# An attention and feed-forward kernel with its weight decode partly moved to GpSimd, 14 scratch slots and a new order of steps

## The chip, the core and the metric

The kernel runs on one core of a Trainium2 chip. The metric is device time in microseconds of one execution, the median of several runs. The engines are TensorE (PE in the profile; its weight loads are PEld), VectorE (DVE), ScalarE (ACT) and GpSimd (POOL); SyncE (SP) issues the loads, ScalarE the stores.

## The reference

Two stages follow each other, all in 32-bit floats. The first is chunked attention over 4 batches, 8 heads, 768 positions, head size 64, with 8 memory keys in front of every window:

```python
for c in range(nc):                     # chunks of 32 queries
    k_full = concat(mem_k, k[l_start:r_end])   # 16 left, 8 right of the chunk
    v_full = concat(mem_v, v[l_start:r_end])
    a = softmax(scale * q_c @ k_full.T)
    out[c] = a @ v_full
x = out as 3072 tokens x 512
h = x @ w_in                            # 512 x 1024
solu = h * softmax(h)
ln = (solu - mean) / sqrt(var + 1e-6) * g_ln
return ln @ w_out                       # 1024 x 512
```

The two weight matrices arrive as 64-bit floats; the host hands them over as pairs of 32-bit words, and the kernel decodes them itself.

## The kernel before, in words

The 3072 tokens are 24 tiles of 128. A unit is one tile (units 0 and 1) or two (units 2 to 12). The program is a list of steps, the string ORDER, read from left to right; a step name is a kind, its number (unit, tile, piece, with a part behind a point) and, behind @, an engine: V VectorE, S ScalarE, G GpSimd, Y SyncE. Each engine executes its steps in the order of that list and waits where data or a buffer are not there. Nothing else sets the order.

**Weights.** w_in is eight pieces (0 to 7, piece 2c + h is row block c, half h), w_out eight (8 to 15). D loads a piece of 512 KB (L268) into a slot. A (ScalarE, L274) unpacks the high words, B and E (VectorE, L279, L284) shift and mask them to a float and its power of two, H rounds the float into w_in_h or w_out_h. T (VectorE, L301) turns the low words into a float:

```python
nc.vector.scalar_tensor_tensor(t, word(i, 0), factor, p, ALU.mult, ALU.mult)
```

that is integer word times 2^-52 times the power of two. R adds float minus rounded float plus low part on TensorE with three products by an identity matrix (L309, L310, L311), and W (ScalarE) copies the sum to w_in_l. Some w_out pieces are instead scaled, subtracted and added on GpSimd or VectorE (K L319, Y L324, J L328).

**Attention, per unit.** Lq, Lk, Lv load q, k and v (L236). S (TensorE, L400) makes the scores, M the negative row maximum (L422), Bm subtracts it (L431), X is the exponential (ScalarE, L440), Z the row sum and its inverse (L444 to L448). The probabilities are turned on TensorE and copied out (PT L380, PC) or by a transposing transfer with a split into 16-bit halves before and a join after it (Ps, Px L361, Pm; copies of L221 on ScalarE and L223 on GpSimd). V multiplies by v (L400), N scales (L470). The result x is turned the same two ways (XT, or Xs Xx Xm) and divided into a high and a low float (XH, XL L229).

**Feed-forward, per tile.** G multiplies x by w_in in four steps of six products (L509: high times high, high times low, low times high, two halves), needing both halves of one row block. Hm, He, Hu are the maximum (L518), exponential (L523) and product with h and its mean (L533, L536), Sq the squares (ScalarE, L541), C subtracts the mean (VectorE, L551), Dn the inverse deviation (GpSimd, L557 to L560). Us Ux Um (or UT on TensorE) turn the tile, UH and UL make its high and low floats. O multiplies it by w_out in eight steps of three products (L570), Os scales (L578), St stores (L583).

**Buffers.** Scratch tiles are 12 slots of 128 x 1024 floats, handed out and returned in the order of the list, so a load into a slot waits for the last reader of what lay there; 8 "fr" tiles hold rounded floats, three double banks ("two") and two single banks ("one") of PSUM hold products.

## Time and profile before

| what | value |
|---|---|
| three timed runs | 351.1, 352.71, 355.86 us; median 352.71 |
| profiled execution | 352.38 us, span 350.6 us |
| TensorE busy | 338.9 us, 97% of the span |
| VectorE, ScalarE, GpSimd busy | 230.2, 203.4, 201.5 us |
| granted TensorE clock, mean | 0.983 of full speed |
| HBM read, written | 35.52 MB, 6.29 MB |

The profiled execution is 1.78 us longer than its span, which is counted from the first to the last instruction. A busy TensorE is modelled: the ends of pipelined products are estimated, so the length of one product in the timeline (0.39 us) is longer than the distance to the next (0.23 us); sums of TensorE work are read from distances between starts. An engine's instructions start in the order of its list, so what delays one delays all behind it.

### The profile page before, as it was taken

To read this page: it belongs to the slowest core of one execution; us is meant where nothing else is said; L and a number is where in the kernel's file an instruction comes from. 1 tells how busy PE (TensorE), PEld (TensorE's weight loads), DVE (VectorE), ACT (ScalarE), POOL (GpSimd) and SP (SyncE) were. 2 spreads that over 40 slices of the span, in tenths; PEclk is the share of its full clock that TensorE was granted. 3 is DMA by queue.
4 is the path that set the end of the run, shared out by engine and by line. 5 is a ranking of instruction groups with operands and counts; after the bars stand their busy time and mean duration, and the time that the engine had idled before them with its cause. 6 is when DMAs were issued, how large, how long until landed. Compare 5 with 4: busy or idle time off the path is not lost.

```text
span 350.6 us, 9994 instructions
## 1 busy us (share of the span) xinstructions
PE 338.9 (97%) x4368; PEld 269.4 (77%) x4368; DVE 230.2 (66%) x298; ACT 203.4 (58%) x265; POOL 201.5 (57%) x231
## 2 busy tenths in 40 slices
PE   7599999999999999999999999999999999999995
PEld 7367768778778878888888888888888888888884
DVE  2769789999985597386775685687562754846200
ACT  1565596587397586443761756786772626576211
POOL 0020037798786569839859549775655978466100
PEclk9679999999999999999999999999999999999999
DMA  7989893955979639979859796949934335362021
GB/s 230 409 310 407 284 345 118 283 125 113 201 254 190 143 84 194 339 158 166 218 209 197 263 192 153 227 130 169 245 89 68 60 91 107 76 127 53 2 90 60
DMA packets 96907, 62.90 MB, mean 179 GB/s; under 512 B 82528, under 2 KB 82528, under 8 KB 96864
## 3 DMA queue, kind: packets, MB, share of 16 engines
q1 hardware_dynamic: 93408, 55.98, 65.0%
q10 hardware_dynamic: 3456, 6.29, 4.9%
q8 instruction: 34, 0.56, 0.6%
q14 instruction: 9, 0.07, 0.1%
HBM read 35.52 MB, written 6.29 MB: 119 GB/s over the span
## 4 chain that ended last, share of the span: by engine, by line
PE 88%; DVE 7%; DMA 2%; ACT 1%; issue 1%; SPq 0%
PE one L570 39%; PE two L509 35%; PE two L400 9%; PE one L309 2%; DMA slot<-in_w_in 2%; PE two L380 2%; DVE per_row L518 1%; DVE slot L533 1%; DVE slot L470 1%; DVE slot L551 1%; DVE fr L301 1%; DVE fr L229 1%; PE one L310 1%; PE one L311 1%; SPq L236 0%
## 5 line engine op out<-in xcount | busy, mean ns | idle before, releaser
L223 POOL TENSOR_SCALAR slot<-slot 128x1024 uint16<-128x1024 uint16 x94 | 119.5, 1297 | 53.6 <-DVE slot L551 16.2
L570 PE MATMUL one<-w_out_h,fr 128*128 128x512 f32 x384 | 133.8, 399 | 0.0
L509 PE MATMUL two<-w_in_h,fr 128*128 128x512 f32 x384 | 133.4, 398 | 0.3 <-ACT two L541 0.3
L509 PEld LDWEIGHTS two<-w_in_h,fr 128*128 128x128 f32 x384 | 72.2, 188 | 17.8 <-ACT two L541 0.5
L570 PEld LDWEIGHTS one<-w_out_h,fr 128*128 128x128 f32 x384 | 72.2, 188 | 17.6
L221 ACT COPY slot<-slot 128x1024 uint16<-128x1024 uint16 x62 | 71.7, 1195 | 15.7 <-DVE slot L551 10.0
L509 PE MATMUL two<-w_in_l,fr 128*128 128x512 f32 x192 | 75.7, 394 | 0.0
L570 PE MATMUL one<-w_out_l,fr 128*128 128x512 f32 x192 | 75.7, 394 | 0.0
L518 DVE TENSOR_REDUCE per_row<-two 128x1 f32<-128x1024 f32 x24 | 29.3, 1222 | 41.0 <-PE two L509 41.0
L229 DVE TENSOR_TENSOR fr<-slot,fr 128x1024 fp32r<-128x1024 f32 x30 | 45.6, 1526 | 6.0 <-PE one L570 2.1
L523 ACT ACTIVATE slot<-two,per_row 128x1024 f32<-128x1024 f32 x24 | 26.8, 1116 | 38.8 <-DVE per_row L518 36.5
L509 PEld LDWEIGHTS two<-w_in_l,fr 128*128 128x128 f32 x192 | 36.2, 188 | 8.1
L570 PEld LDWEIGHTS one<-w_out_l,fr 128*128 128x128 f32 x192 | 36.1, 188 | 8.0
L578 ACT ACTIVATE o_sb<-one,per_row 128x512 f32<-128x512 f32 x24 | 16.4, 685 | 34.5 <-PE one L570 34.5
L541 ACT ACTIVATE two<-slot,per_row 128x1024 f32<-128x1024 f32 x24 | 26.8, 1118 | 13.9 <-DVE per_row L536 13.8
L533 DVE CUSTOM_DVE_ANT_0 slot<-two,slot 128x1024 f32<-128x1024 f32 x24 | 29.2, 1215 | 8.1 <-ACT slot L523 8.0
L551 DVE TENSOR_SCALAR slot<-slot,per_row 128x1024 f32<-128x1024 f32 x24 | 23.2, 965 | 11.1 <-ACT two L541 11.1
L470 DVE TENSOR_TENSOR slot<-two,per_head 128x1024 f32<-128x1024 f32 (+1 forms) x13 | 14.8, 1140 | 11.3 <-PE two L400 11.3
L400 PEld LDWEIGHTS two<-v,slot 64*32 64x32 f32 x1536 | 16.6, 108 | 5.6 <-issue 4.8
L319 POOL TENSOR_SCALAR slot<-slot,g_col 128x512 f32<-128x512 f32 x4 | 3.3, 821 | 29.7 <-DVE slot L284 28.1
L400 PE MATMUL two<-v,slot 64*32 64x64 f32 x1536 | 19.0, 232 | 0.7 <-issue 0.7
L400 PEld LDWEIGHTS two<-k,q 64*32 64x32 f32 x1536 | 16.4, 105 | 4.3 <-issue 3.3
(67 smaller groups left out, 336.9 us busy)
## 6 DMA issues: line engine op xcount, KB each, us to landing
v<-in_vw SPq DMA_DIRECT2D x11, 1024.0 KB, 7.1
k<-in_kw SPq DMA_DIRECT2D x11, 672.0 KB, 5.2
out<-o_sb ACTq DMA_DIRECT2D x24, 256.0 KB, 2.4
q<-in_qT SPq DMA_DIRECT2D x11, 512.0 KB, 4.8
slot<-in_w_in SPq DMA_DIRECT2D x8, 512.0 KB, 9.1
slot<-in_w_out SPq DMA_DIRECT2D x8, 512.0 KB, 5.6
v<-in_vw SPq DMA_DIRECT2D x2, 512.0 KB, 10.8
k<-in_kw SPq DMA_DIRECT2D x2, 336.0 KB, 4.6
```

Of the source, the lines that this page charges most:

```text
L221: nc.scalar.copy(out, in_)
L223: nc.gpsimd.tensor_scalar(out, in_, 1.0, 0.0, ALU.mult, ALU.add)
L229: either(on).tensor_tensor(out, a, b, ALU.subtract)
L400: nc.tensor.matmul(out[32 * j:32 * j + 32, r, t, g], *pairs(slice(r * D, (r + 1) * D), t, g, j), start=True, stop=True,)
L470: nc.vector.tensor_tensor(x, heads(u, get("xp", u), D).rearrange("p r t g n -> p r (t g) n"), rinv.broadcast_to([P, 2, n, D]), ALU.mult,)
L509: nc.tensor.matmul(h[:, half], x[a], w[b][:, c, half * HALF:(half + 1) * HALF], start=c == 0 and i == 0, stop=c == NC_ - 1 and i == 2,)
L518: nc.vector.tensor_reduce(take("per_row", ("hm", t), 1), flat(get("h", t)), axis=AX.X, op=ALU.max, negate=True)
L523: nc.scalar.activation(take("slot", ("u", t), 3), flat(get("h", t)), AF.Exp, bias=get("hm", t), scale=1.0, accum_out=take("per_row", ("esu ...
L533: nc.vector.tensor_tensor_reduce(u, flat(get("h", t)), u, 1.0, 0.0, ALU.mult, ALU.add, accum_out=usum)
L541: nc.scalar.activation(flat(get("h", t)), get("u", t), AF.Square, bias=get("nmu", t), scale=1.0, accum_out=take("per_row", ("var", t), 1),)
L551: nc.vector.tensor_scalar(u, u, get("nmu", t), None, ALU.add)
L570: nc.tensor.matmul(get("o", t), u[a], w[b][:, f], start=f == 0 and i == 0, stop=f == NF - 1 and i == 2)
```

## The change

It does four things. The number of slots goes from 12 to 14. For pieces 2 to 7 of w_in the step T becomes two, Tc and Tp: Tc turns the low words into floats in place, with the factor (GpSimd for all six), Tp multiplies by the power of two (GpSimd for pieces 4 to 7, VectorE for 2 and 3). The step C takes an engine: GpSimd for tiles 0, 1, 2 and 4, VectorE for the other 20. And the whole list ORDER is written anew, with other engines for some copies: eight of the sixteen H go from ScalarE to GpSimd, 17 of 24 UH are on GpSimd (9 before), 18 of the 16-bit copies of probabilities on GpSimd (25 before), both VectorE scalings K go to GpSimd. The kinds and counts of the TensorE steps are the same. Three further functions (exps_by_head, scaled_max, inverses) are defined and named by no step of the list.

```diff
-SLOTS, ROUNDED = 12, 8
+SLOTS, ROUNDED = 14, 8
...
-CT Lq0@Y Lq1@Y Lk0@Y Lk1@Y Wu16 D0 D1 A0 Lv0@Y S0 D3 Lv1@Y D2 S1 M0 Lg Bm0 D4 M1 X0 A1 Bm1 Z0 Lq2@Y
...
+Lk0@Y CT Lq0@Y Lk1@Y Wu16 Lq1@Y S0 S1 M0 M1 D0 A0 Bm0 B0 D5 Tc5@G Bm1 X0 E0 A5 B5 T0 X1 PT1 D1 A1 D3
+B1 H0@G PT0 Z1 Lv1@Y R0 Tc3@G A3 E1 T1 PC0 D4 Tc4@G E5 B3 PC1 V1 N1 H1@S Z0 R1 Lv0@Y E3 V0 H5@S D2
...
+    def w_word_f32(i, on):
+
+        f = piece(i)[3]
+        factor = g_word[:, f:f + 1] if i in SCALED else 2.0**-52
+        low = word(i, 0)
+        if on == "S":
+            nc.scalar.activation(low.bitcast(F32), low, AF.Copy, scale=factor)
+        else:
+            either(on).tensor_scalar(low.bitcast(F32), low, factor, 1.0, ALU.mult, ALU.mult)
+
+    def w_word_exp(i, on):
+        p = get("a", i)[:, HALF:]
+        t = take("fr", ("t", i), 1)[:, 0:HALF]
+        either(on).tensor_tensor(t, word(i, 0).bitcast(F32), p, ALU.mult)
+        used("raw", i)
...
-    def u_center(t):
+    def u_center(t, on):
         u = get("u", t)
-        nc.vector.tensor_scalar(u, u, get("nmu", t), None, ALU.add)
+        if on == "S":
+            nc.scalar.activation(u, u, AF.Identity, bias=get("nmu", t), scale=1.0)
+        else:
+            either(on).tensor_scalar(u, u, get("nmu", t), 0.0, ALU.add, ALU.add)
         used("nmu", t)
```

In the changed file the line numbers are shifted: loads of pieces are L269, of q, k and v L237, small products L417, transposes L397, R is L326 to L328, G is L553, Tc is L313, Tp L318.

SyncE at the start, first before, from the first piece on (in the order of the list D0 D1 Lv0 D3 Lv1 D2 Lg D4 Lq2 D5 Lk2 D6):

```order
L268 DMA slot_61<-in_w_in 128x1024
L268 DMA slot_62<-in_w_in 128x1024
L236 DMA v_90<-in_vw 128x1024
L268 DMA slot_64<-in_w_in 128x1024
L236 DMA v_91<-in_vw 128x1024
L268 DMA slot_65<-in_w_in 128x1024
L197 DMA g_col<-in_g_ln 128x8
L268 DMA slot_67<-in_w_in 128x1024
L236 DMA q_86<-in_qT 128x2x512
L268 DMA slot_71<-in_w_in 128x1024
L236 DMA k_88<-in_kw 128x2x672
L268 DMA slot_63<-in_w_in 128x1024
```

And the same place now (D0 D5 D1 D3 Lv1 D4 Lv0 D2 Lk2 Lq2 D6 D14):

```order
L269 DMA slot_61<-in_w_in 128x1024
L269 DMA slot_64<-in_w_in 128x1024
L269 DMA slot_67<-in_w_in 128x1024
L269 DMA slot_69<-in_w_in 128x1024
L237 DMA v_92<-in_vw 128x1024
L269 DMA slot_72<-in_w_in 128x1024
L237 DMA v_93<-in_vw 128x1024
L269 DMA slot_61<-in_w_in 128x1024
L237 DMA k_90<-in_kw 128x2x672
L237 DMA q_88<-in_qT 128x2x512
L269 DMA slot_62<-in_w_in 128x1024
L269 DMA slot_63<-in_w_out 128x1024
```

The four pieces in front of v of unit 1 were two before with v of unit 0 between them; v of unit 0 went from third to seventh, and D2 is the first load into a slot that was used already.

TensorE from the first transposes on, first before (PT0 PT1 V0 XT0 V1, then R0 and R1):

```order
L380 MATMUL two_83<-ident,slot_66 128x128 x4
L380 MATMUL two_81<-ident,slot_69 128x128 x4
L400 MATMUL two_82<-v_90,slot_70 32x64 x32
L380 MATMUL two_83<-ident,slot_70 128x128 x4
L400 MATMUL two_81<-v_91,slot_66 32x64 x32
L309 MATMUL one_84<-slot_63,ident 128x512
L310 MATMUL one_84<-w_in_h,eye_neg 128x512
L311 MATMUL one_84<-fr_73,eye 128x512
L309 MATMUL one_85<-slot_68,ident 128x512
```

And now (PT1 PT0 R0 V1 R1 V0 XT1 and the first product of R5):

```order
L397 MATMUL two_85<-ident,slot_65 128x128 x4
L397 MATMUL two_83<-ident,slot_63 128x128 x4
L326 MATMUL one_86<-slot_62,ident 128x512
L327 MATMUL one_86<-w_in_h,eye_neg 128x512
L328 MATMUL one_86<-fr_75,eye 128x512
L417 MATMUL two_84<-v_92,slot_73 32x64 x32
L326 MATMUL one_87<-slot_68,ident 128x512
L327 MATMUL one_87<-w_in_h,eye_neg 128x512
L328 MATMUL one_87<-fr_76,eye 128x512
L417 MATMUL two_83<-v_93,slot_71 32x64 x32
L397 MATMUL two_84<-ident,slot_65 128x128 x4
L326 MATMUL one_86<-slot_66,ident 128x512
```

R0 moved ahead of V1, R1 between V1 and V0. Up to the first G the list goes on, before, with XT1 R3 S2 R2, then G1.0 G0.0 G1.1 G0.1 R4 R5; now with R5 XT0 R3 S2 R2, then G1.0 G1.1 R6 R4 S3 PT2 G1.2 R7.

GpSimd behind the making of the identity matrix, first before (factors, two diagonal matrices, the first scaled w_out piece):

```order
L200 TENSOR_SCALAR g_word<-g_col 128x8
L204 TENSOR_SCALAR diag<-ident,g_col 128x128
L205 TENSOR_SCALAR diag_r<-ident,g_col 128x128
L319 TENSOR_SCALAR slot_62<-slot_62,g_col 128x512
L324 TENSOR_TENSOR slot_62<-slot_62,w_out_h 128x512
```

And now, ahead of all of that (Tc5 H0 Tc3 Tc4 Tp5 Tc2 Tc6 Tp6 H6 Tp4 Tc7 Tp7):

```order
L313 TENSOR_SCALAR slot_64<-slot_64 128x512
L224 TENSOR_SCALAR w_in_h<-slot_62 128x512
L313 TENSOR_SCALAR slot_69<-slot_69 128x512
L313 TENSOR_SCALAR slot_72<-slot_72 128x512
L318 TENSOR_TENSOR fr_77<-slot_64,slot_66 128x512
L313 TENSOR_SCALAR slot_61<-slot_61 128x512
L313 TENSOR_SCALAR slot_62<-slot_62 128x512
L318 TENSOR_TENSOR fr_75<-slot_62,slot_64 128x512
L224 TENSOR_SCALAR w_in_h<-slot_64 128x512
L318 TENSOR_TENSOR fr_77<-slot_72,slot_73 128x512
L313 TENSOR_SCALAR slot_71<-slot_71 128x512
L318 TENSOR_TENSOR fr_78<-slot_71,slot_74 128x512
```

Twelve instructions of 128 x 512 stand on GpSimd where none stood.

## Rows read from the trace of the kernel before

**Rows 1.** The page's first part: the span, and busy time, share and instructions of each engine.

```profile
span 350.6 us, 9994 instructions
PE 338.9 (97%) x4368; PEld 269.4 (77%) x4368; DVE 230.2 (66%) x298; ACT 203.4 (58%) x265; POOL 201.5 (57%) x231
```

**Rows 2.** The timeline of TensorE: start and length in us, line, operation, out and in, shapes, count; in brackets idle time before it. First PT0, PT1, V0, XT0, then S2, the first G, two R, and the last O.

```profile
10.89 0.93 PE L380 MATMUL two<-ident,slot 128*128 128x128 f32 x4 [2.67 <-ACT slot L440]
13.03 1.12 PE L380 MATMUL two<-ident,slot 128*128 128x128 f32 x4 [1.21 <-ACT slot L440]
14.08 1.19 PE L400 MATMUL two<-v,slot 64*32 64x64 f32 x64
16.05 1.12 PE L380 MATMUL two<-ident,slot 128*128 128x128 f32 x4 [0.79 <-DVE slot L470]
...
24.30 1.48 PE L400 MATMUL two<-k,q 64*32 64x64 f32 x128
...
27.14 0.39 PE L509 MATMUL two<-w_in_h,fr 128*128 128x512 f32 x1
...
32.71 1.02 PE L309 MATMUL one<-slot,ident 128*128 128x512 f32 x2
...
34.04 1.02 PE L309 MATMUL one<-slot,ident 128*128 128x512 f32 x2
...
346.52 0.40 PE L570 MATMUL one<-w_out_h,fr 128*128 128x512 f32 x1
```

**Rows 3.** All waits of TensorE from 30 us to the end: line that waited, what for, us in total, times, longest.

```profile
PE two L400 <- issue: 0.7, 1, 0.7
PE two L380 <- ACT two L541: 0.7, 1, 0.7
PE two L380 <- DVE slot L470: 0.4, 1, 0.4
PE two L509 <- ACT two L541: 0.3, 1, 0.3
```

**Rows 4.** Stretches of the start: from and to in us, length, busy time and instructions of PE, PEld, DVE, ACT, POOL, then granted clock, DMA share, GB/s.

```profile
10.00:14.00 4.00, 1.90 (x8) 1.28 (x8) 2.82 (x9) 3.05 (x6) 0.00 (x0) 0.63 1.03 413
14.00:18.00 4.00, 3.21 (x133) 2.57 (x132) 3.13 (x8) 1.62 (x3) 0.24 (x1) 0.50 1.03 399
18.00:20.00 2.00, 2.00 (x23) 0.87 (x6) 1.82 (x5) 1.80 (x4) 1.98 (x4) 0.50 0.93 359
20.00:22.00 2.00, 2.00 (x6) 1.21 (x5) 1.64 (x4) 0.89 (x3) 0.17 (x1) 0.67 0.45 132
22.00:24.30 2.30, 2.30 (x11) 1.32 (x9) 0.43 (x1) 2.30 (x5) 0.00 (x0) 1.00 1.01 357
```

**Rows 5.** Loads. First from SyncE's timeline the issues of v of unit 1, D4, k of unit 2 and D6 (start, length); then, from the view of DMA issues in windows that hold these one by one, size and us from issue to landing of the same four; last SyncE's wait before loads of pieces for TensorE.

```profile
4.57 0.79 SPq L236 DMA_DIRECT2D v<-in_vw x1
7.26 0.33 SPq L268 DMA_DIRECT2D slot<-in_w_in x1
13.61 0.38 SPq L236 DMA_DIRECT2D k<-in_kw x1
20.35 0.33 SPq L268 DMA_DIRECT2D slot<-in_w_in x1
...
v<-in_vw SPq DMA_DIRECT2D x1, 512.0 KB, 11.6
...
slot<-in_w_in SPq DMA_DIRECT2D x1, 512.0 KB, 11.5
...
k<-in_kw SPq DMA_DIRECT2D x1, 672.0 KB, 9.4
...
slot<-in_w_in SPq DMA_DIRECT2D x1, 512.0 KB, 3.9
...
SPq L268 <- PE one L309: 8.6, 2, 5.2
```

**Rows 6.** The timeline of the start: unpacking of piece 0 as it lands, the subtraction and the exponential of unit 1.

```profile
9.52 0.69 DVE L431 TENSOR_TENSOR slot<-two,per_head 128x512 f32<-128x512 f32 x1
9.57 0.66 ACT L274 ACTIVATE slot<-slot 128x512 f32<-128x512 f32 x1 [7.35 <-DMA slot<-in_w_in]
...
12.35 0.63 ACT L440 ACTIVATE slot<-slot 128x512 f32<-128x512 f32 x1
```

**Rows 7.** Groups of VectorE over the whole span. The first two are by shape (busy us, mean ns, idle before); the last two are one line's instructions (count, shortest, median and longest in ns, first and last start).

```profile
L551 DVE TENSOR_SCALAR slot<-slot,per_row 128x1024 f32<-128x1024 f32 x24 | 23.2, 965 | 11.1 <-ACT two L541 11.1
L301 DVE SCALAR_TENSOR_TENSOR fr<-slot,slot 128x512 fp32r<-128x512 uint32 x10 | 6.7, 685 | 0.1
...
L279 DVE TENSOR_SCALAR slot<-slot x16: 364/417/1262, 11.8 to 77.2; 128x512 uint32<-128x512 uint32 x16
L301 DVE SCALAR_TENSOR_TENSOR fr<-slot,g_word,slot x6: 733/744/1601, 57.3 to 85.5; 128x512 fp32r<-128x512 uint32 x6
```

**Rows 8.** Two lines of GpSimd, shortest, median and longest in ns: scaling of a w_out piece (one tensor in) and its subtraction (two).

```profile
L319 POOL TENSOR_SCALAR slot<-slot,g_col x4: 692/762/1067, 48.2 to 78.9; 128x512 f32<-128x512 f32 x4
L324 POOL TENSOR_TENSOR slot<-slot,w_out_h x6: 1280/1370/1747, 49.8 to 81.0; 128x512 f32<-128x512 f32 x6
```

**Rows 9.** Two later stretches, columns as in Rows 4.

```profile
50.00:60.00 10.00, 9.28 (x254) 6.99 (x254) 9.81 (x19) 6.69 (x11) 6.70 (x9) 1.00 0.57 209
60.00:80.00 20.00, 19.36 (x268) 15.37 (x251) 19.79 (x26) 13.82 (x21) 16.89 (x23) 1.00 0.76 188
```

## The prediction

> **What bounds the kernel now.** I read the page's first part, then the waits of TensorE, then its timeline around the places where it waits. The profiled execution took 352.38 us, 1.78 more than its span; the median of the three timed runs is 352.71, so the two stand 0.33 apart. All sums below are made against 352.38.

> TensorE is busy for 97% of the span [rows 1]. From the first product of x with w_in at 27.14 to the last product with w_out at 346.5 the only waits are four, 0.7, 0.7, 0.4 and 0.3 us, 2.1 us together [rows 2, 3]. So the span is three pieces: a start of 27.1 us, a full TensorE with 2.1 us of holes, and a tail of 4 us behind the last product. The change alters no TensorE step in kind or number (the step names count up to the same 192 O, 96 G, 10 R, 26 S and V, 11 transposes), so the full stretch can lose its holes and nothing else. All the rest must come from the start: work done before 27.14 that used to be done after it.

> [...] TensorE does its first transposes at 10.89 and 13.03 and its first V at 14.08 with holes between, and works without a hole from 16.05 on [rows 2]. [...] And the loads come one behind the other: v of unit 1 is issued at 4.57 and lands 11.6 later at 16.2, the seventh block of the row (D4) at 18.8, k of unit 2 at 23.0 [rows 5].

> **The change, part by part.**

> *Order of loads.* The first sixteen loads are shuffled on SP. I give each load the landing time that its place in the row had before: v of unit 1 stays fifth behind the four small ones, 16.2; v of unit 0 takes D4's place, 18.8; q of unit 2 takes k's place, 23.0. D6 keeps its place. Before, its issue waited until 20.35, 5.2 us of it for the product R that freed its slot, and the DMA share fell to 0.45 between 20 and 22 [rows 4, 5]. With 14 slots it still waits for a product (R0), but R0 now stands before V1. D14 behind it waits for the row sum of unit 0 (about 19), and behind that stand D10, D7 and the loads of unit 3; R7 needs D7 only at 36. No TensorE wait after 27 names a load [rows 3], so what the loads gain or lose there is hidden behind TensorE's own work; I cost it at nothing. If that cover fails, the next late load is q of unit 3 before S3, and each microsecond it is late counts in full.

> *Start of TensorE.* Now PT1 is first. The row maximum of unit 1, the subtraction (0.69) and its exponential (0.63) lie behind piece 0's shift on VectorE, which waits for ScalarE's unpacking from 9.57 to 10.23 [rows 6]: shift to 10.6, subtraction to 11.3, exponential to 12.0. From 12.0 the list PT1 PT0 R0 V1 R1 V0 XT1 R5 XT0 R3 S2 R2 then has no hole that I can find (v lands at 16.2 and 18.8, before the engine has done PT1, PT0, R0 and then V1, R1). Before, XT0 V1 R0 R1 XT1 R3 S2 R2 took the 11.1 us from 16.05 to 27.14. The new list has these eight and PT1, PT0 (1.12 each at the low clock), V0 (1.19) and R5 (1.33, the distance of two R at full clock) [rows 2].

> If the low clock lasts as long into the list's work as before, G1.0 starts at 12.0 + 11.1 + 4.8 = 27.9. If the clock comes back as many microseconds sooner as the unbroken work starts sooner (4), 4 us of low clock become 2 us: 25.9. S2 alone sets the same end: 23.0 + 1.5 + 1.3 = 25.8. The rows show the clock low where TensorE had holes and full after unbroken work, but not which of the two holds it down, so both ends stay; I take 27.0, near the middle. [...]

> At 27.0 one R more is done than before, so this part is worth 0.14 + 1.33 = 1.5 us (0.6 to 2.7).

> *Low words on GpSimd.* Six pieces lose the 0.685 us product on VectorE [rows 7]; each gets a one-input pass (Tc) on GpSimd, and four get the second product (Tp) there too, two keep it on VectorE. No row shows a pass from 32-bit integers on GpSimd. The nearest rows for 128x512 are the one-input scaling, 0.69 to 1.07, and the two-input subtraction, 1.28 to 1.75 [rows 8]; I take 1.07 for Tc (it reads with a stride and converts), 1.37 for Tp, and keep 0.69 and 1.75 as ends. The binding place is R6: D6 at 24.3, then Tc6, Tp6 and a copy (H6, as the scaling): 24.3 + 1.07 + 1.37 + 0.8 = 27.5, at the upper end 28.9. TensorE comes to R6 after G1.0 and G1.1, twelve products of the 24 that took 5.57 us [rows 2], at 29.8. Queued behind Tc6 while it waits for its load are Tp6, H6 and Tp4; R4 needs Tp4, and comes after R6. It is covered at both ends by G1.0 and G1.1: nothing. Past 2.3 us of extra cost every further microsecond is TensorE's.

> *Centring on GpSimd for four tiles, more copies there.* Each takes 0.97 us off VectorE [rows 7]. Three of the centrings and four of the low-word products stand, before, ahead of the first w_out product: 3 x 0.97 + 4 x 0.685 = 5.6 us less on VectorE there. This matters because VectorE was busy for 9.8 of the 10 us from 50 and 19.8 of the 20 from 60, and three of TensorE's four waits lie there [rows 3, 9], 0.72 + 0.37 + 0.27 = 1.4 us. The one of 0.72 at issue is not VectorE's. I take half of the 2.1 us as gone, 1.1, since I can bound the rest only from both sides: a list whose steps stand as close to their users can open new holes; ends are 2.1 gone and none.

> *Later order, tail.* After 110 us TensorE never waits before, so a better order there gains nothing; the last product, its scaling and its store stand as before. I cost both at nothing.

> Sum: 352.38 - 1.5 - 1.1 = 349.8; with the 0.33 to the median, **350.0**. Ends of this case: 352.38 - 2.7 - 2.1 = 347.6 and 352.38 - 0.6 = 351.8.

> **Rivals.**

> *VectorE is held up beside GpSimd (0.27).* VectorE's shift takes 0.36 to 1.26 us, the low-word product 0.73 to 1.60 [rows 7]: the long ones stand where GpSimd works too. GpSimd had almost nothing to do before 27 us, now it has the decode. Place: from V0's end (about 20) to the low half of x for G1.0, VectorE has N0, two Tp, four shifts or masks and XL1, about 4.4 us, ready at 24.6 to 25, so 2 us of cover. If six of these run at their longest, 6 x 0.87 = 5.2, so 3.2 are not covered, and G1.0 slips to 30: 353.2. It decides when more than two of the six are hit. Against it: GpSimd has two or three instructions in that stretch. The same hold-up after 50 us gives back the 1.1: together 352 to 355. [...]

> *The integer pass on GpSimd is slow (0.07).* This is the case on the slower side. GpSimd's list up to R7's low word is six Tc, four Tp and two copies: 6x + 4 x 1.37 + 2 x 0.8 = 6x + 7.1. It can start when the second piece lands, about 10.9 (the first at 9.57 [rows 6], and one block of 1.3, half of what lies between 16.2 and 18.8), and TensorE comes to R7 at 27.0 + 2.8 + 2.7 + 1.5 + 0.9 + 1.4 = 36.2. So it decides at x = 3.0 us; at 5 us TensorE waits 12 us in all: 362. Over 2% slower needs x = 4.7, over four times the one-input row. For it: no row has this conversion. Against: the one-input row is 0.69 to 1.07, and even two inputs take no more than 1.75 [rows 8].

> *The clock is back early and VectorE's room removes all holes (0.09).* 25.9 and 2.1 gone: 347.6, with run scatter 346.5.

> *The extra slots don't help.* D6 may still wait for a product as before; since no load is waited for after 27, this moves no number and is part of the forecast.

> **How the numbers follow.** Forecast 0.55, hold-up 0.27, slow pass 0.07, early clock 0.09, and 0.02 for more than the start can give. The range 347.2 to 354.6 holds the forecast, most of the hold-up and half of the early clock, about 8 in 10. Two per cent is 7 us, about what a measurement of this kernel (351.1 to 355.9 in three runs) can tell from no change. Faster than 345.7 would need more than both ends of the start and all holes, 0.03; slower than 359.8 needs the slow pass or a long wait that I have not seen, 0.06; the same 0.91.

> **What would show it.** First product with w_in at 26 to 28 with five R before it, against four at 27.14; the clock row 16 to 20 above 0.5 (early clock) or not; Tc near 1.07; TensorE's waits after 27 us summing to about 1 us and none naming GpSimd; VectorE's stretch 50 to 80 below full. Wrong if Tc is above 3 us, if a wait of several us names a load or a transposing transfer that the new SP order puts behind another, or if TensorE has holes between 12 and 16 and the clock stays low past 22.

## The result, and the profile after

The changed kernel takes 356.07 us (median of 14 runs, 353.54 to 356.96) against 352.84 for the kernel before in the same job: ratio 1.0092, 95% interval 1.007 to 1.0114. By the 2% bound that is no change, and it is slower by more than the runs scatter. The forecast of 350.0 and its range up to 354.6 were too low. The profiled execution took 355.33 us.

The page's first and third part after the change [rows 1]:

```profile
span 353.4 us, 10017 instructions
...
PE 339.2 (96%) x4368; PEld 269.9 (76%) x4368; DVE 230.5 (65%) x289; ACT 201.5 (57%) x260; POOL 223.3 (63%) x251
...
q8 instruction: 34, 0.56, 0.6%
```

TensorE's busy time is the same as before (339.2 against 338.9); the span is 2.8 longer. The last row is the queue that the page names instruction: 34 packets, 0.56 MB, 16 KB each. Its timeline at the places of [rows 2]: PT1 and PT0, R0, S2, first G, S3, PT2 in two rows, V2, last O.

```profile
13.11 1.94 PE L397 MATMUL two<-ident,slot 128*128 128x128 f32 x8 [4.85 <-ACT slot L457]
14.84 1.91 PE L326 MATMUL one<-slot,ident 128*128 128x512 f32 x2
...
24.52 1.48 PE L417 MATMUL two<-k,q 64*32 64x64 f32 x128
...
27.36 0.39 PE L553 MATMUL two<-w_in_h,fr 128*128 128x512 f32 x1
...
32.88 1.48 PE L417 MATMUL two<-k,q 64*32 64x64 f32 x128
34.29 0.55 PE L397 MATMUL two<-ident,slot 128*128 128x128 f32 x3
37.28 0.71 PE L397 MATMUL two<-ident,slot 128*128 128x128 f32 x5 [2.44 <-issue]
...
42.25 1.48 PE L417 MATMUL two<-v,slot 64*32 64x64 f32 x128
...
349.31 0.40 PE L617 MATMUL one<-w_out_h,fr 128*128 128x512 f32 x1
```

All its waits from 30 us on [rows 3]:

```profile
PE two L397 <- issue: 2.4, 1, 2.4
PE two L417 <- issue: 1.2, 1, 1.2
PE two L417 <- POOL slot L224: 0.9, 1, 0.9
```

And stretches with the columns of [rows 4]: length, PE, PEld, DVE, ACT, POOL, granted clock, DMA share, GB/s.

```profile
14.00:18.00 4.00, 4.00 (x43) 2.32 (x43) 2.89 (x8) 3.59 (x7) 1.67 (x3) 0.50 1.02 403
18.00:20.00 2.00, 2.00 (x53) 1.11 (x36) 1.33 (x3) 0.23 (x1) 1.52 (x2) 0.97 1.04 408
...
39.00:42.00 3.00, 3.00 (x7) 1.53 (x5) 1.42 (x1) 0.69 (x2) 2.92 (x5) 0.50 0.21 79
42.00:43.00 1.00, 1.00 (x77) 0.75 (x78) 0.00 (x0) 0.64 (x2) 0.32 (x1) 0.99 0.28 49
```

The first G comes at 27.36 with R5 done, 0.22 later than before and one R (1.33) further: the start is worth 1.11. Then TensorE stops in the middle of PT2, behind three of eight transposes of one step. Nothing that the profile can name holds it, and three transposes of the same step had just run. Behind that hole its clock falls to 0.50 from 39 to 42.

The sums close. From the first G to the end, before: 350.6 - 27.14 = 323.46; less 2.08 of holes and one R, 320.05. After: 353.4 - 27.36 = 326.04, which is 5.99 more: 4.46 of holes (2.44 + 1.16 + 0.86) and 1.53, the three microseconds at half the clock. So, between these two executions, -1.11 at the start, +2.38 in holes, +1.53 in the clock: +2.8.

### The profile page after: what moved, and what is told of

Its sections match the earlier page's. It is cut to its first block, busy times and chain, and to the rows that moved or that the text cites. A ratio compares the mean times of both kernels' runs of the same rounds, so it can differ in the third digit from the quotient of the medians.

```text
span 353.4 us, 10017 instructions
## 1 busy us (share of the span) xinstructions
PE 339.2 (96%) x4368; PEld 269.9 (76%) x4368; DVE 230.5 (65%) x289; ACT 201.5 (57%) x260; POOL 223.3 (63%) x251
## 4 chain that ended last, share of the span: by engine, by line
PE 87%; DMA 4%; DVE 3%; issue 2%; POOL 2%; ACT 1%; SPq 1%
PE one L617 38%; PE two L553 34%; PE two L417 8%; PE one L326 3%; DMA slot<-in_w_in 2%; PE two L397 2%; DMA v<-in_vw 1%; POOL slot L598 1%; PE one L327 1%; PE one L328 1%; SPq L237 0%; SPq L378 0%; POOL slot L224 0%; ACT two L585 0%; DVE per_head L439 0%
## 5 line engine op out<-in xcount | busy, mean ns | idle before, releaser
L224 POOL TENSOR_SCALAR slot<-slot 128x1024 uint16<-128x1024 uint16 x84 | 113.0, 1370 | 48.0 <-DVE slot L598 25.1
L553 PE MATMUL two<-w_in_h,fr 128*128 128x512 f32 x384 | 134.8, 399 | 0.0
L222 ACT COPY slot<-slot 128x1024 uint16<-128x1024 uint16 x72 | 83.2, 1192 | 29.4 <-DVE slot L598 11.0
L553 PEld LDWEIGHTS two<-w_in_h,fr 128*128 128x128 f32 x384 | 72.3, 189 | 17.6 <-DVE fr L230 0.4
L553 PE MATMUL two<-w_in_l,fr 128*128 128x512 f32 x192 | 76.0, 396 | 0.0
L562 DVE TENSOR_REDUCE per_row<-two 128x1 f32<-128x1024 f32 x24 | 29.3, 1219 | 27.5 <-PE two L553 27.4
L553 PEld LDWEIGHTS two<-w_in_l,fr 128*128 128x128 f32 x192 | 36.2, 189 | 8.0
L617 PEld LDWEIGHTS one<-w_out_l,fr 128*128 128x128 f32 x192 | 36.2, 188 | 7.9
L224 POOL TENSOR_SCALAR fr<-slot 128x1024 fp32r<-128x1024 f32 x22 | 25.4, 1155 | 17.5 <-PE one L617 4.7
L598 DVE TENSOR_SCALAR slot<-slot,per_row 128x1024 f32<-128x1024 f32 x20 | 18.9, 956 | 4.0 <-ACT two L585 4.0
L417 PEld LDWEIGHTS two<-v,slot 64*32 64x32 f32 x1536 | 16.3, 106 | 6.3 <-issue 3.3
L417 PEld LDWEIGHTS two<-k,q 64*32 64x32 f32 x1536 | 16.4, 105 | 5.8 <-issue 4.5
L417 PE MATMUL two<-k,q 64*32 64x64 f32 x1536 | 18.8, 225 | 1.3 <-issue 1.2
## 6 DMA issues: line engine op xcount, KB each, us to landing
v<-in_vw SPq DMA_DIRECT2D x2, 512.0 KB, 11.1
```

Of the source, the lines that this page charges most:

```text
L222: nc.scalar.copy(out, in_)
L224: nc.gpsimd.tensor_scalar(out, in_, 1.0, 0.0, ALU.mult, ALU.add)
L417: nc.tensor.matmul(out[32 * j:32 * j + 32, r, t, g], *pairs(slice(r * D, (r + 1) * D), t, g, j), start=True, stop=True,)
L553: nc.tensor.matmul(h[:, half], x[a], w[b][:, c, half * HALF:(half + 1) * HALF], start=c == 0 and i == 0, stop=c == NC_ - 1 and i == 2,)
L562: nc.vector.tensor_reduce(take("per_row", ("hm", t), 1), flat(get("h", t)), axis=AX.X, op=ALU.max, negate=True)
L598: either(on).tensor_scalar(u, u, get("nmu", t), 0.0, ALU.add, ALU.add)
```

## Experiments

All ratios are to the kernel before, timed on the same chip. C is the centring, "hole" a wait of TensorE that names no releaser (issue).

**Is it the work given to GpSimd?** GpSimd after the change, shortest, median, longest in ns: Tc, Tp and C.

```profile
L313 POOL TENSOR_SCALAR slot<-slot x6: 649/670/804, 11.8 to 30.2; 128x512 f32<-128x512 uint32 x6
...
L318 POOL TENSOR_TENSOR fr<-slot,slot x4: 1303/1313/1321, 17.7 to 32.2; 128x512 fp32r<-128x512 f32 x4
...
L598 POOL TENSOR_SCALAR slot<-slot,per_row x4: 3712/3728/4527, 52.3 to 95.5; 128x1024 f32<-128x1024 f32 x4
```

The decode is cheap. C takes 3.7 us where VectorE took 0.97 [rows 7]. Three kernels undo these one at a time.

*e_center_v*: C of tiles 0, 1, 2 and 4 back on VectorE.

```diff
-C0@G ... C1@G ... C2@G ... C4@G
+C0@V ... C1@V ... C2@V ... C4@V
```

> The changed kernel with one thing undone: the centring of tiles 0, 1, 2 and 4 is on VectorE again (0.96 us each) and not on GpSimd (3.9 us each in the changed kernel's trace). Theory 1 (TensorE's instructions come late: an instruction packet arrives at 34.5 to 35.0 us and TensorE, which has run out of instructions at 34.8, goes on at 37.3; the low clock from 39 to 42 follows from this hole): the 2.4 us hole inside PT2 and the low clock stay, only the 0.9 us wait of V4 for GpSimd at 74.7 goes; about 0.9 us less than the changed kernel, ratio to before about 1.0065. Theory 2 (the slow centring is the main loss, since everything behind it on GpSimd is late): 3 us or more come back, ratio about 1.000 or below. Theory 3 (VectorE needs the room): new holes between 45 and 80 us, ratio 1.010 or above.

356.83, ratio 1.0137 (1.0115 to 1.0159): the hole is there as theory 1 has it, but the time is not; 1.010 or above was theory 3's. V4 no longer waits for GpSimd. The first G came early, at 25.77, which the edit (behind 50 us) can't have done; in this execution the clock was back from 15 on:

```profile
15.00:18.00 3.00, 2.61 (x70) 1.47 (x69) 2.18 (x5) 3.00 (x7) 1.47 (x3) 1.00 1.02 414
```

The hole in PT2 grew to 3.86 and ended at 37.10, nearly where the changed kernel's ended (37.28), and a new one of 1.31 came at 78.41. That is between 45 and 80, where theory 3 wants one, but it too waits at issue; VectorE is named there for 0.27 alone. The earlier start only made the hole in PT2 longer.

*e_one_step*: the decode in one step again.

```diff
-Tc5@G ... Tp5@G ... Tp3@V
+T5 ... T3
```

> The changed kernel with the decode in two steps undone alone: Tc is left out and each low word is made in one product on VectorE, as in the kernel before, at the place in the order where the second step stood; the rest of the new order stays. Theory (order of steps against instruction supply, the two-step decode is harmless): VectorE gets four products of 0.69 us back in the start, G1.0 comes 0 to 1 us later, the hole in PT2 still ends at 37.1 to 37.3, and the time stays at 356 within 1 us (ratio to before 1.006 to 1.012). Rival (the two-step decode on GpSimd costs the time, by holding VectorE up): ratio 1.000 to 1.003.

356.31, 1.0103 (1.0083 to 1.0123); hole in PT2 4.16. The two-step decode costs nothing that this can tell.

*e_add_mult*: the form of C on GpSimd.

```diff
-either(on).tensor_scalar(u, u, get("nmu", t), 0.0, ALU.add, ALU.add)
+either(on).tensor_scalar(u, u, get("nmu", t), 1.0, ALU.add, ALU.mult)
```

> The changed kernel with the centring on GpSimd written as (u + minus mean) * 1.0 in place of (u + minus mean) + 0.0. If the 3.9 us of the centring on GpSimd come from its form with two additions, it falls to about 1.4 to 2 us (scaling 128x512 takes 0.69 to 0.79, twice that for 1024 columns), and the wait of 0.86 us of V4 for GpSimd goes; if it is the width or the operand from a column of numbers, it stays at 3.9. Time: 355 to 356 either way, since the hole in PT2 and the low clock behind it don't depend on it.

355.41, 1.0088 (1.006 to 1.0116). GpSimd's row of C, as above:

```profile
L598 POOL TENSOR_SCALAR slot<-slot,per_row x4: 1118/1120/1945, 53.0 to 94.1; 128x1024 f32<-128x1024 f32 x4
```

With a second addition the same instruction took 3.3 times as long as with a multiplication. The time moves by less than the intervals: C is not where it is lost, and the hole in PT2 is there at 3.91.

**Does TensorE wait for its own instructions?** In the changed kernel the only packet of the instruction queue that starts between 28.5 and 39 lies here (the DMA view from 34.5 to 35.0: packets, MB, share), 2.3 us before PT2 goes on:

```profile
q8 instruction: 1, 0.02, 13.9%
```

*e_s3_late*: S3 and the steps on its scores behind V2 and G1.3.

```diff
-E7 S3 Z2 ... PT2 M3 ... Bm3 B9 V2 K10@G N2 G1.3 Hm1 ... G0.0 X3 G0.1
+E7 Z2 ... PT2 ... B9 V2 K10@G N2 G1.3 S3 Hm1 M3 ... G0.0 Bm3 G0.1 X3
```

> The changed kernel with the scores of unit 3 (256 TensorE instructions in 1.4 us) moved from in front of PT2 to behind V2 and G1.3, and the row maximum and the subtraction behind them. Theory 1 (instruction supply): TensorE reaches the end of its instructions about 3 us later, when the packet of 34.5 to 35 is there, so the hole inside PT2 goes; the next packet may be late in S3 by 0 to 2 us; 1 to 3.5 us less than the changed kernel, ratio about 1.000 to 1.006. Rival (PT2 itself waits for something): a hole of 2.4 us stays at PT2, ratio 1.009.

356.04, 1.011 (1.009 to 1.013). PT2 runs through as expected, but the time missed: two waits for VectorE came, 0.71 and 0.97, and the hole is in S3:

```profile
43.22 0.42 PE L417 MATMUL two<-k,q 64*32 64x64 f32 x21 [2.56 <-issue]
```

*e_warm_hole*: eight warming products (32 instructions) behind S1, where TensorE is idle.

```diff
-S0 S1 M0 M1
+S0 S1 Wu8 M0 M1
```

> The changed kernel with eight more warm-up products of zeros (32 more TensorE instructions) right behind S1, where TensorE has nothing to do from 8.3 to 13.1 us. Theory 1 (instruction supply): each packet is asked for 32 instructions sooner in the program, the one that was late about 2 us sooner (in S2 rather than in G1.1), so the hole inside PT2 shrinks from 2.4 us to about 1 us or goes, and the low clock behind it with it: 3 us less than the changed kernel, ratio about 1.000, and another 0.5 to 1.5 us less if the clock stays high through 11 to 17 us. Rival (the hole is a wait for data or a bank that the profile does not name): the hole stays 2.4 us at the same step; at most the start gains, ratio about 1.006 to 1.009.

358.14, 1.0154 (1.0116 to 1.0193), a miss: no faster, though the profiled execution's clock stayed up until 172.5. The holes are 1.08 at 29.78, 2.63 in S3 and 3.27 at 171.9: they moved. Only behind the last did the clock fall:

```profile
173.00:175.00 2.00, 2.00 (x7) 1.52 (x6) 0.00 (x0) 0.00 (x0) 0.36 (x1) 0.50 1.03 423
```

*e_extra_load*: two loads of 256 KB, whose data nobody uses, behind Lg.

```diff
-Lv2@Y Lg H7@S
+Lv2@Y Lg Ld0 Ld1 H7@S
```

> The changed kernel with two more loads of 256 KB each right behind the load of g (issued at about 25 us), into output buffers that are not yet used; nothing reads them. 512 KB are 1.3 us of the DMA engines. Theory 1a (the instruction packet stands in line with the loads that were issued before it): the packet comes about 1.3 us later and the hole inside PT2 grows from 2.4 to about 3.7 us, ratio about 1.013. Theory 1b (instructions come late, but they do not stand behind the loads): the hole stays 2.4 us, ratio 1.009.

355.38, 1.0091 (1.007 to 1.0112). The hole is 3.79 against 2.44, and the packet began at 35.95 instead of 34.98. That looks like theory 1a, but the run does not show it: e_center_v, e_add_mult and e_one_step, with no load added, have holes of 3.86, 3.91 and 4.16 and packets at 34.69, 35.62 and 36.15. The time is theory 1b's.

```profile
38.47 1.02 PE L400 MATMUL two<-ident,slot 128*128 128x128 f32 x5 [3.79 <-issue]
```

**A count that fits all of them.** The windows' rows give how many products and weight loads TensorE had begun when it stopped; number 954 below is the 954th of them, and an edge is a count at which TensorE can stop. Changed kernel, and b_shift64 below:

```profile
0.00:36.90 36.90, 28.83 (x603) 21.46 (x604) 24.87 (x50) 18.84 (x32) 11.89 (x21) 0.91 0.96 356
```

```profile
0.00:29.00 29.00, 22.04 (x476) 17.78 (x477) 17.12 (x37) 12.26 (x21) 3.19 (x12) 0.86 0.88 319
```

| kernel and hole | products + weight loads begun |
|---|---|
| e_warm_hole 29.78; b_shift64 29.77; e_shift64_am 28.98; e_shift128_am 31.74 | 953, 953, 954, 954 |
| after 37.28; e_center_v, e_extra_load, e_add_mult, e_hold_d8, e_hold_d9, e_hold_w7_am | 1207 each |
| e_one_step, b_s3_early, e_order_b, e_order_b_am; e_warm_hole 37.44 | 1208 each |
| e_s3_late 43.22; e_hold_d8 40.64; e_g_first_am 46.01 | 1462, 1462, 1463 |

Whatever stood there in the order, TensorE stopped at 954, 1207 or 1462 or one beside, some 255 apart. (The expectations of e_order_b, b_s3_early and e_g_first_am still put the edges at 1217 and 1473.) Later holes fit too: the one of e_center_v at 78.41 stands at 2735, six times 254.7 behind 1207, the one of 1.16 at 179.32 in the changed kernel stands at 5789, 18 times 254.6 behind 1207, and the wait of 0.72 in the kernel before [rows 3] at 3502, nine times 255.

```profile
0.00:178.10 178.10, 168.74 (x2894) 132.32 (x2895) 138.14 (x180) 107.40 (x143) 125.81 (x132) 0.97 0.84 241
```

The 18 traces have 40 waits of TensorE at issue of 0.6 us or more: each stands within four instructions of such an edge and ends 2.2 to 2.6 us behind the start of a packet. Shorter ones need not be of this kind: six of 0.26 to 0.58 near 95.9 to 101.1 stand at one step, number 3186 (3218 in e_warm_hole, with its 32 more), off the edges and 8.4 to 8.7 us behind a packet; their cause is open.

```profile
q8 instruction: 1, 0.02, 11.8%
```

That the packet is asked for when TensorE enters the one in front of it is my inference from such pairs. If the edges are put every 254.55 from 445 on (where e_shift128_am has a hole, at 14.69), and the entry is the start of the first product or weight load there, the 18 traces have 595 pairs of an entry and the next packet: in 133 the packet started 1 to 48 instructions ahead of the entry (106 of them inside G or O), so it can be asked for some tens of instructions earlier. In the others other transfers matter: where they kept the DMA engines busy for under a fifth of the time between, the packet started 0.74 to 1.18 us behind the entry (the middle 80% of 115, none over 1.51); where for four fifths or more, 0.90 to 3.75 (of 280, median 2.4, longest 6.55). That agrees with packets standing in line with loads.

**Three tests of that.**

*b_s3_early*: the kernel before, one step moved.

```diff
-G0.1 R4 R5 D9 Z2 S3
+G0.1 S3 R4 R5 D9 Z2
```

> The kernel before with one step moved: S3 stands in front of R4 and R5 instead of behind them (256 small instructions of TensorE 2.7 us earlier), all else the same. Theory: number 1217 is reached at about 35.5 in place of 37, and the packet of 34.4 is usable at 36.6, so a hole of about 1 us with no releaser (issue) opens in R5, R6 or at the first G after them, which this kernel did not have; 353 to 354, ratio 1.001 to 1.004, more if the clock falls behind it. Rival (TensorE's instructions are not what it waits for): no hole there, ratio 0.999 to 1.001.

352.86, 1.0027 (1.0 to 1.0054), as expected, with a hole that this kernel did not have:

```profile
37.51 1.13 PE L309 MATMUL one<-slot,ident 128*128 128x512 f32 x2 [1.67 <-issue]
```

*b_shift64*: the kernel before, 64 useless instructions in idle time, order and data untouched.

```diff
+def tiny(n):
+    z_ps = free["two"][-1][0:32, 0, 0:64]
+    for _ in range(n):
+        nc.tensor.matmul(z_ps, z[0:64, 0:32], z[0:64, 0:64], start=True, stop=True)
...
-S1 M0 Lg
+S1 Wt16 M0 Lg
```

> The kernel before with 64 useless instructions of TensorE (16 small products of zeros, each two products and two weight loads) put behind S1, where TensorE sits idle from 8 to 10.9; nothing else. Theory (a packet of 256 is fetched when TensorE enters the packet in front of it, 3 to 6 us pass until it can be used, and a step S or V of two tiles runs through a whole packet in 1.4 us): the edge of a packet now falls on both ends of S2 (from 24.3), so the one behind S2 is asked for at its start and usable some 5 to 6 us later: a hole without a releaser of 3 to 4.4 us at 26 to 30, by the same reckoning further ones of 1.5 to 2 near 67, 133 and 166; 355 to 360, ratio 1.008 to 1.022. Rival (the holes belong to the order of the steps, or 64 instructions in idle time are harmless): no hole there, ratio 0.999 to 1.002.

357.5, 1.0145 (1.012 to 1.017). The first transposes start 0.4 later, V0 and XT0 earlier than before; the hole is where the count put it, and the clock is low around its end and behind it (windows as above):

```profile
29.77 1.87 PE L314 MATMUL one<-slot,ident 128*128 128x512 f32 x2 [4.32 <-issue]
```

```profile
24.00:28.00 4.00, 1.45 (x129) 1.47 (x129) 3.23 (x6) 0.66 (x2) 0.00 (x0) 0.95 0.94 348
28.00:32.00 4.00, 2.23 (x4) 1.10 (x4) 1.44 (x3) 0.00 (x0) 0.00 (x0) 0.50 1.02 408
```

The further holes that I reckoned for 67, 133 and 166 did not come; only the first edge was right. So the kernel before is fast also because its edges lie well: order, data and loads are the same here.

*e_shift128_am* and *e_shift64_am*: the changed kernel with the cheaper C and Wt32 or Wt16 behind S1.

> The changed kernel with the centring on GpSimd as (u + minus mean) * 1.0, and with 128 useless instructions of TensorE behind S1, in its idle time from 8.3 to 13.1; order unchanged. Theory (edges of packets): an edge now falls in the middle of S3 and of V2 in place of their ends; the packet that PT2 needed is asked for before the first G, and PT2 runs without a hole; by the same reckoning a hole of up to 0.9 near 30 and one below 1 near 58 or 220; no low clock from 39 to 42. 356.07 - 0.9 - 2.4 - 1.5 + 1.5 = 352.8, ratio 0.997 to 1.004; PT1 may start up to 1 us later, if the packet for it is late. Rival (holes belong to the order): the hole of 2.4 to 3.9 in PT2 stays, 355.4 or more.

> As the run before with 64 useless instructions instead of 128. Theory: as in the kernel before with 64, the edges fall on the ends of S2: a hole of some 3 us at 26 to 29.5 in front of the first G or inside G1.0, further ones of 1 to 2 us near 65 and 130; 357 to 361, ratio 1.013 to 1.025. Rival: as e_add_mult, 355.4, with the hole in PT2.

359.37, 1.0187 (1.0145 to 1.0229), and 360.01, 1.0241 (1.02 to 1.0281). The first is with 128, a miss, the second with 64, as reckoned in the start: 3.91 at 28.98, and none in PT2; the further ones came at 101.8 and 174.9, not near 65 and 130. With 128 the hole in PT2 is gone, but one of 3.32 at 14.69 held up everything behind it, one of 3.69 came at number 954 inside S2, and further ones of 1.03 and 1.96. Removing the hole at one edge made one at the next.

**Can the packets come earlier?** Three kernels let SyncE wait for a piece of w_in_l, by a transfer of one column out of it: *e_hold_d8* before D8, *e_hold_d9* with Hd2 before D9, *e_hold_w7_am* with Hd7 and then D8 and D13 behind W7, and the cheaper C.

```diff
+def hold(i):
+    c, half = divmod(i, 2)
+    nc.sync.dma_start(free["o_sb"][0][:, 0:1], w_in_l[:, c, half * HALF:half * HALF + 1].bitcast(F32))
...
-W4@S D8
+W4@S Hd4 D8
```

> The changed kernel, in which SyncE first waits for the low part of w_in's piece 4 (about 33.6 us) before it issues D8 and all loads behind it (D8, D13, q and v for the next units). The data and the order of everything else are the same. Theory (TensorE waits for its own instructions, 16 KB packets of 256 that stand in line behind the loads): D8 to v were in the queues when the fourth packet was asked for (between 25.5 and 28 us in the changed kernel); without them the packet starts up to 3.9 us earlier than 34.98, the hole of 2.44 us in PT2 goes, and with it the low clock from 39 to 42; 356.07 becomes 352 to 353, ratio 0.998 to 1.002. If only loads that were issued before 25.5 stand ahead of the packet, nothing changes: the hole stays at 2.4, 356. Rival (the hole is TensorE's own sequencer and no transfer): hole 2.4, 356. A wait for D8, which now comes some 8 us later, would show as a hole naming a load or R8 after 50 us; neither theory counts on it.

354.39, 1.0044 (1.0016 to 1.0073), above the 352 to 353 expected, but the best median of a changed kernel. Its profiled execution was its fastest, 351.96 (others up to 357.67): there the clock stays up and the packet starts at 31.82, 0.7 behind number 954 in place of 2.1. Some of that can be scatter: e_s3_late and e_g_first_am have 0.8 and 0.9 with nothing held. Two holes are left in the start, 1.28 and 1.60; the second packet started 4.0 behind its entry, probably behind the loads that were let go at 32:

```profile
34.34 0.71 PE L401 MATMUL two<-ident,slot 128*128 128x128 f32 x5 [1.28 <-issue]
...
40.64 0.34 PE L421 MATMUL two<-v,slot 64*32 64x64 f32 x15 [1.60 <-issue]
```

> As the run before, but SyncE waits earlier, before D9, for the low part of piece 2 (about 28 us): D9, v of unit 2, g and everything behind them are issued after 28. Theory (instruction packets behind loads): more loads are out of the packet's way, the hole in PT2 is gone or below 0.5 us even if the packet is asked for as early as 25.5; 352 to 353 unless v of unit 2, issued some 3 us later, is itself late for V2 (then a wait for a load at V2, each microsecond counting in full). Rival (no transfer has a part in the hole): 2.4 us hole, 356.

355.57, 1.0088 (1.0066 to 1.0109). A miss: the packet came at 35.94, 3.7 behind number 954, and the hole was 4.30. e_center_v, e_add_mult and e_one_step, with nothing held, have 3.4, 3.4 and 3.7, so this run tells nothing of the loads that it held.

> The changed kernel with three things: SyncE waits for the low part of piece 7 (about 38 us) before D8, D13 and what stands behind them (in the run held before D8 it waited until 31.8, and the fifth packet then came only at 38.4, behind the loads that were let go at 32); the centring on GpSimd is (u + minus mean) * 1.0; nothing else. Theory (packets stand in line behind loads): the fourth packet at about 31.8 as there, hole in PT2 1.3; the fifth then meets no load and comes before 36, so the 1.6 us hole in V2 goes; no low clock; V4's wait goes. 354.39 - 1.6 - 0.7 = 352.1, ratio 0.995 to 1.002. Rival (the packets come when TensorE asks for them and loads matter little): the fifth at 38 or later, the hole in V2 stays, 353.5 to 354.5. Loads that are issued at 38 could be late for S4 or V3 after 50; that would show as a wait for a load.

355.2, 1.0066 (1.0041 to 1.0091), a miss in time. The packets came as the theory has them (33.42 and, with the queues empty, 37.09; V2 ran through), yet PT2 kept a hole of 1.29, and a new wait of 2.30 at PT3 for VectorE's low half of x appeared. The DMA engines from 36 to 37, the second last column:

```profile
36.00:37.00 1.00, 1.00 (x8) 0.91 (x8) 1.00 (x2) 0.29 (x1) 0.52 (x1) 1.00 0.00 0
```

That packet started 1.1 us behind its entry and the one after it 1.2; in the changed kernel, with loads there, these are 1.9 and 3.4. This is the nearest to a test of the loads by an edit. For the packet of PT2 3.2 us still pass from number 954 (32.67) to the first instruction behind 1207 (35.89), and S3 runs through a packet in 1.4.

**Another order?** *e_order_b* puts TensorE's list between R4 and PT3 back into the sequence of before (G0.0 G0.1 S3 G1.2 G0.2 R7 PT2 G0.3 V2 G1.3 XT2), *e_order_b_am* adds the cheaper C, and *e_g_first_am* puts seven G steps and V2 ahead of S3.

> The changed kernel with TensorE's list between R4 and PT3 put back into the sequence of the kernel before (G0.0 and G0.1 ahead of S3, then G1.2 G0.2 R7 PT2 G0.3 V2 G1.3 XT2); everything ahead of R4 and behind PT3 as changed. Theory (1217 instructions are there until some 2.2 us behind the fourth packet, 1473 until as much behind the fifth, whatever the order): TensorE then reaches number 1217 at the end of S3 at about 37, when the packet of 35 is usable, so the hole is 0 to 0.5 in place of 2.44 and no low clock follows; 356.07 becomes 351.5 to 353.5, ratio 0.997 to 1.003. Rival (the loss is spread over the new list, VectorE and the late loads, and S3 is only where it shows): the hole or a wait for VectorE comes back elsewhere, 355 to 356.5.

> The run before together with the centring on GpSimd as (u + minus mean) * 1.0, which took 1.12 us in place of 3.73. By the theory 0.5 to 1 us less than the run before, 351 to 352.5, ratio 0.995 to 1.000, if V4's wait for GpSimd goes; by the rival 355 to 356.

> The changed kernel with long products in front of small instructions: seven of the eight G steps of the first two tiles, R7 and PT2 stand ahead of S3, and V2 before that (TensorE: G1.0 G1.1 R6 R4 G0.0 G0.1 G1.2 R7 PT2 G1.3 V2 G0.2 S3 XT2 G0.3 G2.0 PT3 S4), and centring as in the run before. Theory (1217 instructions until some 2.2 us behind the fourth packet, 1473 behind the fifth): number 1217 is reached in V2 at 41.5, well behind 37.2, number 1473 in S3 at 44, behind 41.5; no hole without a releaser before 48 and no low clock. What the later S3 costs (M3 Bm3 X3 PT3 behind it) would show as waits for VectorE after 46, 1 to 2.5 us; 351 to 354, ratio 0.995 to 1.005. Rival (holes come in any new order, whatever the count): issue holes of 2 us or more before 48, 356.

358.72 (1.0176, 1.0135 to 1.0217), 357.66 (1.0147, 1.0108 to 1.0186) and 359.73 (1.02, 1.0173 to 1.0227): all missed. In the first two the hole moved into S3 and was still 1.8 and 1.6: TensorE comes there 0.8 and 0.4 us earlier than in the kernel before, and the packet 1.0 and 1.2 later (35.42 and 35.61). And my list opened a wait of 4.16 at PT3, behind VectorE (the step XL2 late). In the third the hole at 1207 is gone, but 1.29 came at 1463 and 3.31 for VectorE. The order of before alone does not bring its time back; these three test my hand-made orders as much as the theory.

## Why the prediction was wrong

**The step that failed** is the sentence that the full stretch "can lose its holes and nothing else" and that "all the rest must come from the start": from it the later order was costed at nothing, and 1.1 us of holes were taken as gone. It held TensorE to wait for data and buffers alone. I had seen the wait of 0.72 at issue [rows 3] and set it aside as not VectorE's. It was the one row of the trace of before that showed the mechanism; the queue of 34 instruction packets stood in the same page. The holes came to 4.46 instead of about 1, and the clock behind the largest cost 1.53 more. The case of a "long wait that I have not seen" had 0.06 and was given only to the side over 2%. None of the signs of being wrong that I had listed came.

**The start** was right in kind and size: G1.0 at 27.36 for 27.0, five R done; -1.11 for -1.5. Its working was off in both parts: the list began at 13.11, not 12.0, since the exponential of unit 1 came later, and the clock came back by 18 to 20 (0.97), earlier than at 20 to 22. That one execution hit 27.0 so closely is partly luck: in eleven kernels whose list up to there is the changed one's, the first G came at 27.12 to 27.36 in the five where the clock rose at 18.0 to 18.5, and at 25.57 to 26.82 in the six where it rose at 14.9 to 17.5. The two ends of the forecast, 25.9 and 27.9, were much like two kinds of execution of the same list; what brings the clock back no run shows. But the start could not pay: TensorE reached number 1207 at 34.6, 2 us sooner than before, and waited for a packet that came when it had come before (34.98 against 34.37). e_center_v shows the same in an execution whose start was 1.6 us better still.

**Order of loads at nothing**: no wait names a load, as predicted, and the cover that I named was the wrong one. What loads can delay, as far as the runs show it, is the packet (in the tally a median of 2.4 us behind the entry among other transfers, 0.74 to 1.18 with few; in e_hold_w7_am 1.1 and 1.2 for 1.9 and 3.4).

**Decode on GpSimd at nothing**: right. Tc is 0.67 for 1.07 taken, Tp 1.31 for 1.37; R6 never waits, and undoing it gains nothing.

**Centring on GpSimd** was counted as 0.97 off VectorE and never priced on GpSimd; it is 3.73 there, 15.7 us in four. Its visible price is V4's wait of 0.86.

**VectorE's relief of 5.6 us**: its own waits on TensorE's list did go (no wait names VectorE or ScalarE now), the 1.4 us that the prediction meant. VectorE is hardly emptier from 50 to 80, 9.67 and 19.69 against [rows 9]:

```profile
50.00:60.00 10.00, 10.00 (x200) 7.95 (x199) 9.67 (x14) 6.37 (x11) 6.21 (x4) 1.00 0.80 299
60.00:80.00 20.00, 19.08 (x453) 15.07 (x431) 19.69 (x24) 12.61 (x18) 17.34 (x12) 1.00 0.65 152
```

**The rivals.** VectorE held up beside GpSimd gave a time near the result (352 to 355) by the wrong mechanism. Longer times on VectorE are there: the plain low-word product now takes 788 ns in the mean (685 before), the longest shift 1415 (1262 before); that GpSimd is their cause no run shows. But TensorE never waits for VectorE, and taking the GpSimd work away (e_one_step, e_center_v) gains nothing. The slow integer pass is excluded by 0.67 us. The early clock came in six other executions (above); five of them took 356.0 to 359.3 all the same, the sixth is that of e_hold_d8. The spread that I read as a sign of GpSimd agreed only in part: of the five shifts of before beside which GpSimd was busy for two thirds of the time or more, one was long.

**Open:** which loads stand before a packet, and by how much. From number 954 to the packet's start 2.1, 3.2, 3.4, 3.4 and 3.7 us passed in executions with the loads in their place or two more, 0.8 in e_s3_late; a hold before D8 gave 0.7, one before D9 3.7. In eight of the twelve changed kernels without added products the packet started within 0.6 us of the landing of v of unit 2, in four 0.7 to 2.4 us ahead of it; no run tells why. No version beats the kernel before.

## What to carry to other kernels

In a kernel with many small TensorE instructions, count them along the order: here, where a run of them passed through some 255 products and weight loads faster than the next packet came (3 to 9 us at the holes up to 46 us), TensorE stopped, whatever the data did. A hole of a microsecond that names no releaser is worth reading as a late instruction packet: the count of instructions at which it stands, taken from a windows row, and a packet's start 2.2 to 2.6 us ahead of its end show whether it is one. Here a gain ahead of such a point was lost to the wait for the packet: 1.11 us at the first G of the changed kernel, then 2.44 of hole in PT2.

## What the hardware showed that I had not expected

- 64 useless TensorE instructions in idle time cost 5 us (b_shift64): with them an edge between instruction packets lay at the end of a dense step, and a hole of 4.32 stood there.
- From the start of a packet to its first instruction, when TensorE waited for it, 2.2 to 2.6 us passed in all 40 cases. With other transfers on the DMA engines for under a fifth of the time between, a packet that did not start ahead of TensorE's entry into the one in front of it started 0.74 to 1.18 us behind (the middle 80% of 115).
- On GpSimd, adding a column and then 0.0 to 128x1024 floats took 3.73 us, adding it and multiplying by 1.0 took 1.12.
- The length of a hole alone did not tell whether the clock falls. Behind one of 2.44 us it went to 0.50 for about 3 us of work, and behind 1.96 (e_shift128_am at 61.03) and 2.00 (e_add_mult at 179.79, the row below) as well; behind 2.56 (e_s3_late), 2.63 (e_warm_hole) and 2.39 (e_shift64_am at 174.86) it did not fall, nor behind 1.28 and 1.60 (e_hold_d8).

```profile
181.40:184.70 3.30, 3.30 (x9) 2.58 (x8) 3.27 (x6) 1.65 (x3) 0.00 (x0) 0.50 1.03 231
```
